# The first phase in an order from a list scheduler, smaller first weight chunks, and the loop's reads in an output bank

## Chip, cores, metric

One core of one Trainium2 chip. The time is device microseconds of one execution; every run in this study was in the fast state, except two of e2's and one of e4b's, which count as slow because they lie over 1.5% above the fastest run of their kernel; ratios leave them out. The profile is one execution, so its span and its waits are one sample; the timed runs are several.

## The reference, cut to what matters

```python
# x: 8 batches x 8 heads x 512 tokens x 64; state: 8 x 8 x 32 x 64
scores  = scale * x @ state.T                    # softmax over the 32 states
xread   = a @ state                              # 512 rows per batch
scores2 = scale * state @ x.T                    # softmax over the 512 tokens
sread   = a2 @ x                                 # 32 rows per batch
tokens  = concat([xread, sread])                 # 8 heads side by side: 512 columns
gate = max(tokens @ w_gate, 0)                   # 512 -> 1536
val  = tokens @ w_val
out  = (gate * val) @ w_out                      # 1536 -> 512
```

The kernel never forms `xread`. For each batch it multiplies the state by the weights (U, 256 rows by 2 x 1536) and multiplies U by the transposed softmax weights (ANS), which saves a product.

## The kernel before

There are five engines in play: TensorE (PE), VectorE (DVE), ScalarE (ACT), GpSimd (POOL) and SyncE (SP, the queue of most DMAs). Each has its own instructions, and the kernel fixes their order. It is written as an explicit order: a list `FIRST` for batches 0, 1 and the preparation of batch 2, then a loop over batches 2 to 7.

A step `("g", b, jf)` is one of the twelve 128-column blocks of gate and value of batch b (four matmuls); `("ge", b, jf)` is its relu on ACT and multiply on DVE. `("u", b, lo, n)` are the U matmuls for n columns, `"ue"` their evictions. `"w"` and `"wo"` load weight chunks, `"xl"` a batch of x, `"st"` states. `"x_bar"` and `"a_bar"` are DMA transposes: of the converted x (xT<-xb), and of the softmax weights (ans<-a_sn). `"sc"`, `"exp"`, `"sum"`, `"mul"` are scores and softmax, `"sr"` the state reads, `"out"` a third of an output tile, `"dummy"` matmuls on a warm-up tile that are meant to keep the clock up.

```python
FIRST = [
    ("st", 1, 2), ("w", 0, 512, ("s", 0)), ("dummy", 7), ("st_cast", 0, 1, "v"), ("st_mm", 0, 1),
    # ... cut
    ("mul", 0, 0, 1, 1, "v"), ("w", 512, 1024, ("v", 0)), ("exp", 0, 1, 0, 1), ("sc", 0, 1, (1,)),
    # ... cut
    ("xl", 3, 0, 8, ("o", 8)), ("u", 0, 1024, 256), ("ge", 1, 7), ("ue", 0, 1024, 256, 0, "a"), ("g", 1, 2),
    # ... cut
    ("u", 1, 1280, 256), ("ge", 1, 9), ("xl", 2, 0, 8, ("v", 512)), ("ue", 0, 1280, 256, 0, "a"), ("sr", 0),
    # ... cut
    ("ue", 2, 512, 512, 3, "v"), ("ue", 2, 512, 512, 1, "v"), ("out", 1), ("conv", 3, 0, 4, "p"), ("u", 2, 1024, 512),
    ("conv", 3, 4, 4, "v"), ("xc", 3, 0, 2, "p"), ("xc", 3, 2, 2, "p"), ("sc", 2, 1), ("sc", 2, 0), ("xl", 4),
    ("x_bar", 3), ("out", 1), ("out", 1), ("exp", 2, 0), ("exp", 2, 1), ("ue", 2, 1024, 512, 1, "a"), ("out", 1),
    ("out", 1), ("sum", 2), ("mul", 2), ("out", 1), ("out", 1), ("a_bar", 2), ("ue", 2, 1024, 512, 0, "a"),
    ("out", 2), ("sr", 2), ("sre", 2), ("ue", 2, 1024, 512, 2, "a"), ("ue", 2, 1024, 512, 3, "a"),
]
# the last entry of a load is its gate: it is issued after that other load has landed.
# ("o", 8): last third of w_out; ("v", 512): w_val columns 512 to 1023.

ps_r = pool("ps_r", 6, PS)      # six rotating PSUM banks
ps_o = pool("ps_o", 2, PS)      # two for output tiles

def sr_mm(b):                   # reads: 32 small matmuls into one rotating bank
    ps = ps_sr[b] = ps_r.tile([128, 130], FP32, name="sr_ps", tag="r")
    # ... cut

# in the loop, batch s + 1 prepared in batch s, at jf == 8:
    sr_mm(s + 1)
    sr_ev(s + 1)
    u_burst(s + 1, 768, 768, "avavav")   # takes all six rotating banks
```

The softmax here doesn't subtract the row's maximum and nothing guards it: scores larger than these inputs give would overflow.

Of the kernel before, what the change touches and what calls it, by code (L numbers as in the profile page):

```python
# [8 lines left out]
FP32 = mybir.dt.float32  # L9
BF16 = mybir.dt.bfloat16  # L10
# [4 lines left out]


FIRST = [
    ("st", 1, 2), ("w", 0, 512, ("s", 0)), ("dummy", 7), ("st_cast", 0, 1, "v"), ("st_mm", 0, 1),
    ("st_ev", 0, 1, "a"), ("dummy", 2), ("conv", 0, 0, 2, "v"), ("conv", 0, 2, 2, "v"), ("xt", 0, 0),
    ("xe", 0, 0, "v"), ("xt", 0, 1), ("dummy", 3), ("conv", 0, 4, 2, "p"), ("conv", 0, 6, 2, "p"), ("sc", 0, 0, (0,)),  # L20
    ("xe", 0, 1, "a"), ("dummy", 1), ("exp", 0, 0, 0, 1), ("dummy", 3), ("sc", 0, 0, (1,)), ("xt", 0, 2),
    ("dummy", 3), ("sum", 0, 0, 0, 1), ("dummy", 3), ("exp", 0, 0, 1, 1), ("xe", 0, 2, "a"), ("xt", 0, 3),
    ("sc", 0, 1, (0,)), ("sum", 0, 0, 1, 1), ("dummy", 7), ("xe", 0, 3, "v"), ("mul", 0, 0, 0, 1, "p"),
    ("mul", 0, 0, 1, 1, "v"), ("w", 512, 1024, ("v", 0)), ("exp", 0, 1, 0, 1), ("sc", 0, 1, (1,)),
    ("sum", 0, 1, 0, 1), ("dummy", 4), ("xl", 1, 0, 4, ("g", 0)), ("exp", 0, 1, 1, 1), ("mul", 0, 1, 0, 1, "v"),
    ("sum", 0, 1, 1, 1), ("dummy", 7), ("conv", 1, 2, 2, "p"), ("mul", 0, 1, 1, 1, "v"), ("st_cast", 1, 2, "v"),
    ("dummy", 6), ("xl", 1, 4, 4), ("at", 0, 0), ("at", 0, 1), ("ae", 0, 0, "a"), ("st_mm", 1, 1), ("u", 0, 0, 256),
    ("ae", 0, 1, "v"), ("dummy", 8), ("st_ev", 1, 1, "v"), ("ue", 0, 0, 256, 1, "v"), ("u", 1, 0, 256),
    ("ue", 0, 0, 256, 0, "a"), ("ue", 1, 0, 256, 0, "a"), ("ue", 1, 0, 256, 1, "v"), ("g", 0, 0),
    ("conv", 1, 0, 2, "v"), ("ge", 0, 0), ("st", 2, 8), ("u", 0, 256, 256), ("conv", 1, 6, 2, "p"),  # L30
    ("conv", 1, 4, 2, "v"), ("ue", 0, 256, 256, 0, "a"), ("xt", 1, 1), ("g", 0, 1), ("w", 1024, 1536), ("xt", 1, 0),
    ("ue", 0, 256, 256, 1, "a"), ("xt", 1, 2), ("xe", 1, 1, "v"), ("ge", 0, 1), ("xe", 1, 0, "a"), ("xt", 1, 3),
    ("g", 0, 2), ("xe", 1, 3, "v"), ("xe", 1, 2, "a"), ("ge", 0, 2), ("sc", 1, 0), ("sc", 1, 1), ("exp", 1, 0),
    ("wo", 0, 4), ("g", 0, 3), ("dummy", 1), ("exp", 1, 1), ("sum", 1, 0), ("dummy", 6), ("mul", 1, 0, 0, 2, "p"),
    ("dummy", 1), ("wo", 4, 8), ("u", 1, 256, 256), ("dummy", 2), ("sum", 1, 1), ("mul", 1, 1, 0, 2, "v"),
    ("dummy", 5), ("ge", 0, 3), ("at", 1, 0), ("dummy", 1), ("at", 1, 1), ("u", 0, 512, 256),
    ("ue", 1, 256, 256, 1, "a"), ("ae", 1, 0, "a"), ("ae", 1, 1, "v"), ("ue", 1, 256, 256, 0, "v"), ("g", 1, 0),
    ("ue", 0, 512, 256, 0, "v"), ("g", 1, 1), ("ge", 1, 0), ("ue", 0, 512, 256, 1, "a"), ("ge", 1, 1), ("wo", 8, 12),
    ("u", 1, 512, 256), ("g", 1, 3), ("g", 0, 4), ("ue", 1, 512, 256, 1, "v"), ("ge", 1, 3), ("ge", 0, 4),
    ("ue", 1, 512, 256, 0, "a"), ("u", 0, 768, 256), ("ue", 0, 768, 256, 1, "v"), ("g", 0, 5),  # L40
    ("ue", 0, 768, 256, 0, "v"), ("u", 1, 768, 256), ("ue", 1, 768, 256, 0, "v"), ("ge", 0, 5), ("g", 1, 5),
    ("ge", 1, 5), ("g", 0, 6), ("ue", 1, 768, 256, 1, "a"), ("ge", 0, 6), ("g", 1, 4), ("g", 1, 7), ("ge", 1, 4),
    ("xl", 3, 0, 8, ("o", 8)), ("u", 0, 1024, 256), ("ge", 1, 7), ("ue", 0, 1024, 256, 0, "a"), ("g", 1, 2),
    ("ge", 1, 2), ("ue", 0, 1024, 256, 1, "a"), ("u", 1, 1024, 256), ("g", 0, 7), ("g", 0, 8),
    ("ue", 1, 1024, 256, 1, "a"), ("xb_alloc", 2), ("ue", 1, 1024, 256, 0, "v"), ("g", 0, 9), ("ge", 0, 7),
    ("ge", 0, 8), ("g", 1, 6), ("g", 1, 9), ("ge", 0, 9), ("st_cast", 2, 8, "v"), ("ge", 1, 6), ("u", 0, 1280, 256),
    ("u", 1, 1280, 256), ("ge", 1, 9), ("xl", 2, 0, 8, ("v", 512)), ("ue", 0, 1280, 256, 0, "a"), ("sr", 0),
    ("g", 1, 8), ("ue", 0, 1280, 256, 1, "a"), ("st_mm", 2, 2), ("ue", 1, 1280, 256, 1, "a"),
    ("ue", 1, 1280, 256, 0, "a"), ("sre", 0), ("sr", 1), ("u_alloc", 2), ("ge", 1, 8), ("st_ev", 2, 2, "a"),
    ("sre", 1), ("g", 0, 11), ("g", 0, 10), ("at_alloc", 3), ("st_mm", 6, 2), ("ge", 0, 11), ("st_mm", 4, 2),  # L50
    ("st_ev", 6, 2, "v"), ("u", 2, 0, 256), ("conv", 2, 4, 4, "p"), ("ge", 0, 10), ("out", 1), ("g", 1, 10),
    ("ge", 1, 10), ("st_ev", 4, 2, "v"), ("g", 1, 11), ("out", 1), ("ge", 1, 11), ("conv", 2, 0, 4, "p"),
    ("xc", 2, 0, 2, "p"), ("xc", 2, 2, 2, "p"), ("at_alloc", 2), ("xb_alloc", 3), ("ue", 2, 0, 256, 0, "a"),
    ("ue", 2, 0, 256, 1, "a"), ("u", 2, 512, 512), ("ue", 2, 512, 512, 0, "a"), ("u", 2, 256, 256),
    ("ue", 2, 256, 256, 1, "a"), ("x_bar", 2), ("ue", 2, 512, 512, 2, "a"), ("out", 1), ("ue", 2, 256, 256, 0, "v"),
    ("ue", 2, 512, 512, 3, "v"), ("ue", 2, 512, 512, 1, "v"), ("out", 1), ("conv", 3, 0, 4, "p"), ("u", 2, 1024, 512),
    ("conv", 3, 4, 4, "v"), ("xc", 3, 0, 2, "p"), ("xc", 3, 2, 2, "p"), ("sc", 2, 1), ("sc", 2, 0), ("xl", 4),
    ("x_bar", 3), ("out", 1), ("out", 1), ("exp", 2, 0), ("exp", 2, 1), ("ue", 2, 1024, 512, 1, "a"), ("out", 1),
    ("out", 1), ("sum", 2), ("mul", 2), ("out", 1), ("out", 1), ("a_bar", 2), ("ue", 2, 1024, 512, 0, "a"),
    ("out", 2), ("sr", 2), ("sre", 2), ("ue", 2, 1024, 512, 2, "a"), ("ue", 2, 1024, 512, 3, "a"),  # L60
]

@with_exitstack
def kernel(
# [9 lines left out]
    nc = tc.nc  # L74
# [38 lines left out]
    tiny = const.tile([128, 1], FP32, name="tiny")  # L113

    xf, xb, xT, e_sn, cs, rc, asn, ANS, U, hsb = ({} for _ in range(10))
    ps_sc, ps_sr, ps_st, ps_x, ps_a, ps_u, ps_g = ({} for _ in range(7))

    def cp(eng, o, i):
        if eng == "a":
# [158 lines left out]


    def sr_mm(b):  # L280
        ps = ps_sr[b] = ps_r.tile([128, 130], FP32, name="sr_ps", tag="r")
        for c in range(NC):
            for s in range(2):
                for j in range(NJ):
                    nc.tensor.matmul(ps[32 * j:32 * j + 32, 65 * s:65 * s + 65], e_sn[b][:, c, s, j],  # L285
                                     xs(b)[:, c, j, 1 + 65 * s:66 + 65 * s],
                                     start=(c == 0 and s == 0), stop=(c == NC - 1), skip_group_check=True)
# [69 lines left out]
                                 ANS[b][:, :, kc], start=(kc == 0), stop=(kc == 1))  # L357
            ps_g[b, jf].append(ps)

    def gv_ev(b, jf):  # L360
        pss = ps_g[b, jf]
        g_sb = gpool.tile([128, 512], BF16, name="g_sb", tag="g_sb")
        nc.scalar.activation(out=g_sb, in_=pss[0], func=AF.Relu)  # L363
        nc.vector.tensor_tensor(out=hsb[b][:, jf], in0=pss[1], in1=g_sb, op=ALU.mult)  # L364

    def gv(b, jf):
        gv_mm(b, jf)
        gv_ev(b, jf)

    def gvs(jf):  # L370
        f0 = jf * 128
# [7 lines left out]
        nc.scalar.activation(out=g_sb[:, 0:nt], in_=ps[:, 0], func=AF.Relu)  # L379
        nc.vector.tensor_tensor(out=hs[0][:, jf], in0=ps[:, 1], in1=g_sb[:, 0:nt], op=ALU.mult)  # L380

    o_ps = [None]

    def out_piece(b, tsub, q):
        if q == 0:
# [3 lines left out]
        src, t0 = (hsb[b], tsub * 128) if b < B else (hs[0], tsub * 128)  # L389
        for jf in range(4 * q, 4 * q + 4):  # L390
            nc.tensor.matmul(o_ps[0], src[:, jf, t0:t0 + 128], wo_sb[:, jf], start=(jf == 0), stop=(jf == NF - 1))  # L391
        if q < 2:
            return
        ps = o_ps[0]
        o_sb = opool.tile([128, d_model], FP32, name="o_sb", tag="o_sb")
        if b < B:
            cp("av"[tsub % 2], o_sb, ps)
# [26 lines left out]
    def outp(n=1):  # L424
        for _ in range(n):
            p = next(pieces, None)
            if p is not None:
                out_piece(*p)


    ctx.enter_context(tc.manual_schedule())
# [17 lines left out]
    for i in range(3):  # L449
# [3 lines left out]
        "dummy": dummies, "w": w_dma, "wo": wo_dma, "st": st_dma,  # L453
        "st_cast": st_cast, "st_mm": st_mm, "st_ev": st_ev, "conv": x_conv, "xc": x_copy, "xt": x_tr, "xe": x_ev,
        "sc": sc_mm, "exp": sc_exp, "sum": nrm_sum, "mul": nrm_mul, "at": a_tr, "ae": a_ev,
        "u": u_mm, "ue": u_ev, "g": gv_mm, "ge": gv_ev, "gv": gv, "sr": sr_mm, "sre": sr_ev, "out": outp,
        "xb_alloc": xb_alloc, "at_alloc": at_alloc, "u_alloc": u_alloc, "x_bar": x_bar, "a_bar": a_bar, "ub": u_burst, "xl": x_dma,
    }
    for name, *args in FIRST:
# [35 lines left out]
    for s in range(2, B):  # L495
        for jf in range(NF):
            gv(s, jf)
            if jf in (3, 9):
                continue
            outp()  # L500
            for k in ((jf - 1, jf) if jf in (4, 10) else (jf,)):
                aux(s + 1, k)
                nxt(s + 2, k)
            if jf in (2, 8):
                if s + 1 < B:
                    if jf == 2:
                        u_alloc(s + 1)
                    else:
                        sr_mm(s + 1)
                        sr_ev(s + 1)  # L510
                    u_burst(s + 1, 768 * (jf // 8), 768, "avavav")
                outp()
    hs.append(xin.tile([128, NF, B * Ns], BF16, name="hs_sb", tag="xf"))
    for jf in range(NF):
# [34 lines left out]
```

## Time and profile before

| | before |
|---|---|
| median time at first | 235.24 us (3 runs, 234.59 to 237.09) |
| span of the profiled run | 234.0 us |
| PE busy | 95% |
| period of the loop, one batch | 23.58 us |
| effective end of the first phase (second loop batch, at 89.12, less one period) | 65.54 us |

The prediction below shows the lines that carry this. In addition, three lines of the timeline of PE give the head of the kernel. The columns are start and length in us, engine, line, operation, out<-in, shapes and count; in brackets is the idle time just before and what ended it.

```profile
13.48 0.30 PE L304 MATMUL u_ps<-wg_sb,stT 64*32 64x256 bf16 x8
...
15.14 1.04 PE L356 MATMUL gv_ps<-ans,U 128*128 128x512 bf16 x4
...
24.25 0.30 PE L304 MATMUL u_ps<-wv_sb,stT 64*32 64x256 bf16 x8 [0.19 <-DMA wv_sb<-in_moe_w_val_dram]
```

The first weights are used at 13.48, the first step runs at 15.14, and at 24.25 the second pair of weight chunks is met. One line of PE's waits belongs to the hole in front of the loop (released by; us in total, times, longest):

```profile
PE gv_ps L356 <- DMA ans<-a_sn: 2.6, 1, 2.6
```

The transposing DMA of batch 2's weights took 3.51 us from 60.18 on, but PE still had an output piece and the state reads to do until 61.1. It stood still for 2.62 us, and the granted clock was 0.50 from 64 to 67 us.

### The profile page before, as it was taken

The numbers are of one execution on the slowest core, as the hardware profiler recorded it, in microseconds if no ns is written. First come the engines' busy times: TensorE is split into PE (matmuls) and PEld (weight loads), VectorE is DVE, ScalarE is ACT, GpSimd is POOL, SyncE is SP. The second block draws the span as 40 slices with busy tenths as digits, with TensorE's granted clock in tenths as the row PEclk, the third lists the DMA queues.
The fourth block names the chain that finished last, engine by engine and source line by source line (L and its number), as shares of the span: only waits on it lengthen the run. The fifth ranks groups of instructions, "written<-read, shape, count | busy, mean of one in ns | idle before, by whom it ended". The sixth has DMA issues, their size and how long they took to land.

```text
span 234.0 us, 4969 instructions
## 1 busy us (share of the span) xinstructions
PE 222.4 (95%) x2000; PEld 111.8 (48%) x2022; DVE 139.2 (59%) x244; ACT 113.4 (48%) x210; POOL 35.0 (15%) x44
## 2 busy tenths in 40 slices
PE   6999999999599999999999999999999999999993
PEld 3856434534244444444444444444444444586553
DVE  5578888574229674867486748675866535442210
ACT  3457678573246354645463647363736353442121
POOL 3356000083600033003300240000000000000000
PEclk9999999999979999999999999999999999999999
DMA  6999995747901674169415761325131111110132
GB/s 190 173 282 195 207 204 160 227 92 224 275 3 45 148 203 105 48 144 202 112 45 125 216 119 48 90 63 125 45 92 50 49 45 45 45 48 31 60 83 99
DMA packets 39463, 27.85 MB, mean 119 GB/s; under 512 B 21136, under 2 KB 35216, under 8 KB 39440
## 3 DMA queue, kind: packets, MB, share of 16 engines
q1 hardware_dynamic: 34688, 22.81, 35.5%
q0 software_dynamic: 4752, 4.72, 12.5%
q8 instruction: 16, 0.26, 0.5%
q14 instruction: 7, 0.06, 0.1%
HBM read 18.35 MB, written 8.91 MB: 116 GB/s over the span
## 4 chain that ended last, share of the span: by engine, by line
PE 77%; DMA 16%; POOL 2%; issue 1%; ACT 1%; DVE 1%; SPq 0%
PE o_ps L391 35%; PE gv_ps L356 30%; DMA wv_sb<-in_moe_w_val_dram 8%; PE gvs_ps L376 4%; PE u_ps L304 4%; DMA xf<-in_x_dram 4%; DMA xT<-xb 2%; DMA ans<-a_sn 1%; PE sc_ps L241 1%; PE o_ps L413 1%; POOL xb L124 1%; DMA st_f<-in_state_dram 1%; ACT g_sb L363 1%; PE sr_ps L285 1%; POOL wg_sb L152 1%
## 5 line engine op out<-in xcount | busy, mean ns | idle before, releaser
L364 DVE TENSOR_TENSOR h_sb<-gv_ps,g_sb 128x512 bf16<-128x512 f32 x96 | 65.5, 689 | 57.5 <-ACT g_sb L363 53.1
L356 PE MATMUL gv_ps<-ans,U 128*128 128x512 bf16 x384 | 95.8, 382 | 2.6 <-DMA ans<-a_sn 2.6
L391 PE MATMUL o_ps<-wo_sb,h_sb 128*128 128x512 bf16 x350 | 91.2, 381 | 2.0 <-issue 1.2
L363 ACT ACTIVATE g_sb<-gv_ps 128x512 bf16<-128x512 f32 x96 | 57.5, 599 | 61.5 <-PE gv_ps L356 60.7
L356 PEld LDWEIGHTS <-U 128*128 128x128 bf16 x384 | 36.1, 98 | 44.3 <-issue 4.4
L391 PEld LDWEIGHTS <-h_sb 128*128 128x128 bf16 x372 | 35.5, 98 | 43.3 <-issue 4.2
L120 ACT CAST U<-u_ps 128x512 bf16<-128x512 f32 x54 | 28.8, 596 | 3.0 <-PE u_ps L304 2.4
L122 DVE CAST U<-u_ps 128x512 bf16<-128x512 f32 x42 | 26.2, 673 | 1.1 <-PE u_ps L304 1.1
L124 POOL CAST xb<-xf 128x1024 bf16<-128x1024 f32 x11 | 11.2, 1040 | 88.5 <-DMA xf<-in_x_dram 88.5
L120 ACT COPY o_sb<-o_ps 128x512 f32<-128x512 f32 (+2 forms) x20 | 10.8, 538 | 20.5 <-PE o_ps L391 18.2
L122 DVE COPY o_sb<-o_ps 128x512 f32<-128x512 f32 (+2 forms) x18 | 11.4, 635 | 12.7 <-ACT o_sb L120 4.5
L252 ACT ACTIVATE e_sn<-sc_ps 128x512 bf16<-128x512 f32 (+1 forms) x18 | 9.7, 549 | 14.6 <-PE sc_ps L241 14.6
L437 PE MATMUL warm_ps<-warm 128*128 128x256 bf16 x70 | 11.7, 316 | 1.2 <-DVE warm L439 1.2
L124 POOL COPY xs<-xb 128x1024 bf16<-128x1024 bf16 x12 | 12.1, 1040 | 1.6 <-DVE xb L122 1.3
L304 PEld LDWEIGHTS <-stT 64*32 64x32 bf16 x576 | 6.7, 90 | 10.0 <-issue 6.9
L304 PE MATMUL u_ps<-wv_sb,stT 64*32 64x256 bf16 (+1 forms) x288 | 11.2, 306 | 0.2 <-DMA wv_sb<-in_moe_w_val_dram 0.2
L258 DVE TENSOR_REDUCE cs<-e_sn 128x32 f32<-128x1024 bf16 (+2 forms) x12 | 10.2, 852 | 1.7 <-ACT e_sn L252 1.7
L380 DVE TENSOR_TENSOR hs_sb<-gvs_ps,g_sb 128x256 bf16<-128x256 f32 x12 | 5.1, 424 | 9.9 <-ACT g_sb L379 9.9
L304 PE MATMUL u_ps<-wg_sb,stT 64*32 64x256 bf16 (+1 forms) x288 | 10.3, 312 | 0.0
L379 ACT ACTIVATE g_sb<-gvs_ps 128x256 bf16<-128x256 f32 x12 | 4.6, 383 | 10.2 <-PE gvs_ps L376 7.8
L264 DVE TENSOR_TENSOR a_sn<-e_sn,rc 128x1024 bf16<-128x1024 bf16 (+2 forms) x10 | 9.4, 944 | 0.1
L437 PEld LDWEIGHTS <-warm 128*128 128x128 bf16 x70 | 7.2, 112 | 3.4 <-DVE warm L439 1.2
(47 smaller groups left out, 102.5 us busy)
## 6 DMA issues: line engine op xcount, KB each, us to landing
out_dram<-o_sb SPq DMA_DIRECT2D x31, 256.0 KB, 2.4
xf<-in_x_dram SPq DMA_DIRECT2D x6, 1024.0 KB, 6.8
wg_sb<-in_moe_w_gate_dram POOLq DMA_DIRECT2D x3, 512.0 KB, 8.0
wv_sb<-in_moe_w_val_dram POOLq DMA_DIRECT2D x3, 512.0 KB, 9.7
wo_sb<-in_moe_w_out_dram POOLq DMA_DIRECT2D x3, 512.0 KB, 13.3
xf<-in_x_dram SPq DMA_DIRECT2D x4, 256.0 KB, 3.5
xf<-in_x_dram SPq DMA_DIRECT2D x2, 512.0 KB, 4.6
out_dram<-o_sb SPq DMA_DIRECT2D x8, 64.0 KB, 1.7
```

Source lines behind the costliest of these rows:

```text
L120: nc.scalar.copy(out=o, in_=i)
L122: nc.vector.tensor_copy(out=o, in_=i)
L124: nc.gpsimd.tensor_copy(out=o, in_=i)
L252: nc.scalar.activation(out=esl(e_sn, b, kc, j2, n).rearrange("p k j n -> p k (j n)"), in_=ps_sc[b, kc].rearrange("p c s j n -> p (c s) j n ...
L258: nc.vector.reduce_sum(out=c, in_=e, axis=AX.X)
L264: en.tensor_tensor(out=a, in0=e, in1=r.to_broadcast(list(e.shape)), op=ALU.mult)
L304: nc.tensor.matmul(ps[32 * j:32 * j + 32, 0:n], stT[r, b, j, 32 * kc:32 * kc + 32], wsb[w][r, j, lo:lo + n], start=(i == 0), stop=True, sk ...
L356: nc.tensor.matmul(ps.rearrange("p (c t) -> p c t", c=NC), U[b][:, kc, w, f0:f0 + 128], ANS[b][:, :, kc], start=(kc == 0), stop=(kc == 1))
L363: nc.scalar.activation(out=g_sb, in_=pss[0], func=AF.Relu)
L364: nc.vector.tensor_tensor(out=hsb[b][:, jf], in0=pss[1], in1=g_sb, op=ALU.mult)
L391: nc.tensor.matmul(o_ps[0], src[:, jf, t0:t0 + 128], wo_sb[:, jf], start=(jf == 0), stop=(jf == NF - 1))
L437: nc.tensor.matmul(wps[:, 0:cols], warm[:, 0:128], warm[:, 0:cols], start=True, stop=True)
```

## The change

Intent: let a model of all engines order the first phase instead of a person, get the first weights sooner by halving the first chunk, and take the loop's state reads out of the banks that U needs. The core of the diff; the list itself is replaced throughout:

```diff
 FIRST = [
-    ("st", 1, 2), ("w", 0, 512, ("s", 0)), ("dummy", 7), ...
+    ("dummy", 9), ("w", 0, 256, ("s", 0)), ("st_cast", 0, 1, "v"), ("st_mm", 0, 1), ("st", 1, 2),
+    ("xl", 1, 0, 2, ("x", 0, 4)), ("xl", 1, 2, 2), ("xl", 1, 4, 2), ("xl", 1, 6, 2), ("dummy", 2),
     ... cut
+    ("st_ev", 1, 1, "a"), ("sc", 0, 1, (1,)), ("dummy", 2), ("w", 256, 512, ("g", 0)), ("exp", 0, 1, 1, 1),
     ... cut
+    ("gr", 0, 6), ("g", 0, 7), ("gm", 0, 6), ("xl", 2, 0, 8, ("v", 1024)), ("gr", 0, 7), ("st", 2, 8), ("g", 1, 3),
     ... cut
+    ("om",), ("sre", 2), ("mul", 2, 0, 0, 2, "p"), ("ue", 2, 1024, 512, 1, "a"), ("conv", 3, 0, 4, "v"), ("g", 1, 7),
+    ("a_bar", 2), ("xc", 3, 0, 2, "v"), ("xc", 3, 2, 2, "p"), ("at_alloc", 3), ("x_bar", 3), ("xl", 4), ("gr", 1, 7),
+    ("g", 1, 6), ("gm", 1, 7), ("gr", 1, 6), ("g", 1, 5), ("gm", 1, 6), ("gr", 1, 5), ("g", 1, 4), ("gm", 1, 5),
     ... cut
 def sr_mm(b):
-    ps = ps_sr[b] = ps_r.tile([128, 130], FP32, name="sr_ps", tag="r")
+    ps = ps_o.tile([128, d_model], FP32, name="sr_ps", tag="o") if b > 2 else \
+        ps_r.tile([128, d_model], FP32, name="sr_ps", tag="r")
+    ps_sr[b] = ps
-def gv_ev(b, jf):      # relu and multiply together
+def gv_relu(b, jf):    # "gr"
+def gv_mult(b, jf):    # "gm"
     ... output pieces ("om") and their evictions ("oe") are split likewise
 # in the loop
     sr_mm(s + 1)
-    sr_ev(s + 1)
-    u_burst(s + 1, 768 * (jf // 8), 768, "avavav")
+    u_mm(s + 1, 768 * (jf // 8), 768)
+    sr_ev(s + 1)
+    # ... then the six evictions
```

The useful work of the first phase is the same: 24 gate/value steps, all of U for batches 0 to 2, 12 output pieces. Dummies fall from 70 to 33.

## The prediction

> **What bounds the kernel now.** I read the page's busy shares first, then the chain of work that ended last in order of time, then the queue waits, then the engine table in stretches, and last the timeline of one period of the loop. The page says TensorE (PE) is the bound: its three big lines make most of the chain, and the clock is at full speed in 39 of 40 slices.
>
> ```profile
> PE 222.4 (95%) x2000; PEld 111.8 (48%) x2022; DVE 139.2 (59%) x244; ACT 113.4 (48%) x210; POOL 35.0 (15%) x44
> PEclk9999999999979999999999999999999999999999
> PE 77%; DMA 16%; POOL 2%; issue 1%; ACT 1%; DVE 1%; SPq 0%
> ```
>
> "PE 95% busy" hides filler: 70 matmuls on a warm-up tile, and modelled ends. The chain is the better guide. Its 16% DMA all lies before 64 us:
>
> ```profile
> 3.79 9.71 DMA wv_sb<-in_moe_w_val_dram
> 14.60 9.60 DMA wv_sb<-in_moe_w_val_dram
> ...
> 37.58 8.94 DMA xf<-in_x_dram
> 46.56 2.03 POOL xb L124 x2
> 48.61 4.55 DMA xT<-xb
> 53.21 0.64 PE sc_ps L241 x16
> 60.18 3.51 DMA ans<-a_sn
> 63.73 1.87 PE gv_ps L356 x4
> 67.50 0.86 PE gv_ps L356 x4
> 72.93 1.73 PE gv_ps L356 x8
> 96.51 1.73 PE gv_ps L356 x8
> 120.09 1.73 PE gv_ps L356 x8
> ```
>
> Three things are to be seen. PE waits for weight chunks up to 24.2 us. Then batch 2 comes late: its x arrives at 46.5, goes through the conversion, the transposing DMA, scores and weights, and PE stands still from 60.18 to 63.73; the first four matmuls afterwards take 1.87 us where four later take 0.86. And from 72.93 on the loop repeats every 23.58 us (96.51 - 72.93 and 120.09 - 96.51). A period's bare matmul time is 48 gate/value and 48 output matmuls at 0.2157 us (0.86 for four), 20.7, plus U 1.8, scores 0.46, state reads 0.36: 23.3. So the loop is at PE's pace already and **only the first phase has time to give**. The third loop batch starts at 89.12 in the chain; one period earlier is 65.54. That is where the first loop batch would have started on an undisturbed PE, and I call it the effective end of the first phase.
>
> The clock explains the 1.87:
>
> ```profile
> 60.00:65.00 5.00, 2.38 (x40) 0.97 (x39) 1.06 (x3) 0.47 (x2) 3.30 (x4) 0.87 0.92 238
> 65.00:70.00 5.00, 4.78 (x33) 2.30 (x33) 1.38 (x2) 1.97 (x5) 0.00 (x0) 0.79 0.01 3
> ```
>
> The third number from the end is the granted clock. Why batch 2 is late stands in the queue's own waits:
>
> ```profile
> SPq L146 <- DMA wo_sb<-in_moe_w_out_dram: 24.4, 1, 24.4
> ```
>
> The loads of x for batches 3 and 2 sit behind a gate on the last output-weight chunk, until 37.03.
>
> **What the Trainium skill says.** (1) "TensorE: Matmul & The Clock Gate", Part 1: some 3.4 us without PE work halves the clock. The trace agrees: 3.5 us of stillness, then 0.50 granted. (2) "DMA: Bandwidth & Descriptors", Queues, rings and completion order: each DMA engine takes turns between its queue rows. So an x load on the SyncE queue takes about half the engines from the weights on the GpSimd queue while both run. The trace before barely tests this. (3) Same page, Specifications: a minimum of 512 B for line rate. A 256-column chunk writes exactly 512 B of bf16 per row, so it should not fall off a cliff; no run here shows it yet.
>
> **The change, part by part.** Both first phases hold the same useful work: 24 gate/value steps of batches 0 and 1, all of U for batches 0 to 2, and 12 output pieces. So I compare when PE reaches the same state, and what it loses afterwards.
>
> *Smaller first chunks.* Before, the 512-column pair lands at 13.5 us and the first U matmul starts at 13.48. Half of it should land near 12. But the first gate/value step also needs batch 0's weights through ScalarE (ACT). The new order puts four U evictions at 0.59, two transposes' copies at 0.59 in ACT's queue ahead of it: 12.4 + 6 x 0.59 = 15.9, against 15.14 before. So the small chunk alone buys nothing for the first step.
>
> *The state "four steps of batch 0 and four U chunks done, waiting for columns 512 and up"* is met by the kernel before at 24.25, when its second pair lands. In the new order the transfers ahead of that pair are the same, less the state of batches 2 to 7 (0.39 MB, some 1.5 us at 250 to 350 GB/s), less the dip near 12.5 us between the gated pairs, plus up to 0.6 us for twice as many small packets (estimate: a 1 KB packet of x took about 45 ns of an engine at 345 GB/s, a 2 KB one of weights 80 ns at 206 GB/s landed). That gives 22 to 22.5 us. **I take 22.3, a gain of 2.**
>
> *From there to the end.* The kernel before used 24.25 to 60.18, 35.9 us, for 20 steps x 0.863 = 17.3, 8 U chunks x 0.34 = 2.7, U of batch 2 2.0, 12 pieces x 0.863 = 10.4, and some 2.2 of state transposes, scores and reads: 34.6, so 1.3 lost. Then came 5.4 us to the effective end at 65.54: the idle wait and the half-speed clock. The new order loads x of batch 2 behind the third weight pair (27.3 us by 22.3 + 5.1 for 1 MB at 206 GB/s), so x is there near 36, its transpose near 41.5, and its scores stand about 45 us in PE's order. After the issue of the last transposing DMA PE still has four steps, four pieces and a U chunk, 7.5 us, against the 3.5 that it takes. **The 5.4 us should vanish.** New losses: the output weights now share the engines with x of batch 2 and the state. Weights alone would end near 35; sharing 1.4 MB moves that to about 39.5, while PE asks for the third part near 39: estimate 0.6 us. ACT's queue at the head, 0.5; ordinary bank waits, 1.3 again plus 0.3. So 22.3 + 34.6 + 2.7 = 59.6, against 65.54: **5.9 us**.
>
> *Reads in an output bank.* In the loop the reads of the next batch take one of the six rotating banks just ahead of the six that U wants, so U waits:
>
> ```profile
> 107.01 0.10 PEld L304 LDWEIGHTS <-stT 64*32 64x32 bf16 x4 [0.27 <-DVE srn L294]
> 106.37 1.04 PE u_ps L304 x32
> 118.34 0.77 PE u_ps L304 x32
> ```
>
> The burst with the reads ahead of it takes 1.04 us, the other 0.77. Five batches x 0.27 = **1.3 us**, on the path since PE is the bound. The output banks: the piece before closes one and its eviction (0.58) is over before the next piece, 1.3 us later, wants it; the reads take the other.
>
> *The split of relu and multiply and of output piece and eviction* costs no instruction. More multiplications on GpSimd (8 against 2, 0.63 us each) are off the path unless its weight issues (0.75 each) hold them up.
>
> Sum: 5.9 + 1.3 = 7.2; 235.2 - 7.2 = **228.0 us**.
>
> **Rivals.** *Output weights or x of batch 2 become the wait.* If turns favour x, the second and third output pieces stand in PE's order with nothing to pass them, and VectorE's order has the conversion of x ahead of multiplies that PE needs. For: DMA busy at full share up to 35 us with the same bytes. Against: one step of slack is there for each. It would cost 2 to 4 us more: 230 to 232. *ACT becomes the bound between 12 and 35 us.* A step costs relu 0.60, multiply 0.69 and one U eviction of 0.6: 1.9 on two engines, 0.95, against PE's 1.03. So tight that a bad split shows. It would leave the state at 24 and some waits: 230 to 231. *Everything but DMA disappears:* fewer stalls than before, 225 to 226. *Cold clock at the head*, since fillers fall from 70 to 33: PE waits near 9.5 to 12 us with little work. A half clock for a few us of steps: 1 us.
>
> **Range and chances.** The 5.4 us is a clear hole that the order fills, and the loop's 1.3 is nearly sure; the 2 us at the head and the contention are my soft terms, plus or minus 3 together. Time 228.0, range 225.0 to 231.5. Two per cent is 230.5; I give 0.80 to faster, 0.17 to the same, 0.03 to slower (a long wait on a late transfer, with a cold clock after it).
>
> **What would show each step.** In the chain: no long wait for the transposing DMA of batch 2 near the loop's start, and the clock at 1.00 there; the first loop step near 58 to 60 us instead of 63.73; the third U pair of columns met near 22; U bursts of 0.77 in both places and a period of 23.3. A PE wait on the output weights between 36 and 41 would show the first rival; ACT busy over 90% from 13 to 30 with PE waiting on its copies the second. I am wrong if the loop's period grows, or if PE's waits before 58 us sum to more than 8 us after the state is met.

## The result, and the profile after

| | before | after |
|---|---|---|
| median, first comparison | 235.42 us (4 runs, 234.59 to 237.09) | 227.28 us (4 runs, 226.2 to 228.69) |
| ratio, 95% interval | | 0.9649 [0.9574, 0.9724] |
| median, on the chip of the experiments | 236.25 us (13 runs, 235.36 to 236.67) | 227.92 us (6 runs, 226.48 to 228.75) |
| ratio, 95% interval | | 0.9641 [0.9614, 0.9667] |
| span of the profiled run | 234.0 us | 224.4 us |

A ratio is the mean time of one kernel's fast runs over the mean of the other's fast runs of the same rounds, so it is not quite the ratio of the medians. The change is faster by 3.5%.

The page of the kernel after (busy shares, clock, and the shares of the chain that ended last):

```profile
PE 214.4 (96%) x1947; PEld 106.1 (47%) x1969; DVE 140.0 (62%) x246; ACT 117.3 (52%) x218; POOL 37.2 (17%) x47
...
PEclk9999999999999999999999999999999999999999
...
PE 88%; DMA 6%; POOL 2%; SPq 1%; issue 1%; DVE 0%; ACT 0%; POOLq 0%
```

DMA's share of the chain fell from 16% to 6%, and no slice shows a lowered clock (its mean is 1.000). "PE 96%" against 95% says almost nothing: the busy share hardly moves when the kernel gets 3.5% shorter. The chain in order of time (start, length, what):

```profile
13.60 9.00 DMA wv_sb<-in_moe_w_val_dram
22.65 0.52 PE u_ps L311 x24
23.17 4.42 PE gv_ps L363 x20
...
45.22 0.57 PE sc_ps L246 x16
...
50.27 3.45 PE gv_ps L363 x16
...
57.84 0.86 PE gv_ps L363 x4
...
63.49 0.77 PE u_ps L311 x32
...
65.23 1.73 PE gv_ps L363 x8
...
75.09 0.77 PE u_ps L311 x32
...
88.54 1.73 PE gv_ps L363 x8
```

From 22.65 to the last output the chain is PE alone. The scores of batch 2 stand at 45.22 instead of 53.21, and the 3.45 us of steps at 50.27 are four steps of batch 1 (`g(1,7)` to `g(1,4)`) that the new order kept back. Most of them lie ahead of the transposing DMA of batch 2's weights, which takes 3.2 us and is issued here (the length is that of the issue):

```profile
52.85 1.26 SPq L280 DMA_TRANSPOSE ans<-a_sn  x1
```

Beside it run the last of the four steps, output pieces and a U chunk: 5.0 us of work up to the first loop step. That step comes at 57.84 instead of 63.73 and takes 0.86 us, at full clock. Both U bursts are 0.77 us. The period is 88.54 - 65.23 = 23.31.

The engine table in stretches, for the two stretches of the hole and of the low clock in the kernel before. The columns are the stretch, its length, busy time of PE, PEld, DVE, ACT and POOL, then granted clock, DMA share and GB/s:

```profile
60.00:65.00 5.00, 4.84 (x59) 2.28 (x58) 2.74 (x4) 3.54 (x8) 1.94 (x2) 1.00 0.76 262
65.00:70.00 5.00, 5.00 (x25) 2.25 (x23) 5.00 (x9) 2.37 (x5) 2.11 (x3) 1.00 0.14 53
```

PE is busy 4.84 of 5 us where it had been 2.38. The head, from the timeline of PE:

```profile
10.10 0.30 PE L311 MATMUL u_ps<-wv_sb,stT 64*32 64x256 bf16 x8 [0.37 <-DMA wv_sb<-in_moe_w_val_dram]
...
14.23 1.03 PE L363 MATMUL gv_ps<-ans,U 128*128 128x512 bf16 x4
...
22.65 0.30 PE L311 MATMUL u_ps<-wv_sb,stT 64*32 64x256 bf16 x8 [1.78 <-DMA wv_sb<-in_moe_w_val_dram]
...
23.10 4.49 PE L363 MATMUL gv_ps<-ans,U 128*128 128x512 bf16 x20
```

With the two traces side by side the gain splits as follows. The effective end of the first phase after is 81.15 - 23.31 = 57.84, from the start of the loop's second batch.

| stretch | before | after | gain |
|---|---|---|---|
| until columns 512 and up are met | 24.25 | 22.65 | 1.6 |
| from there to the effective end of the first phase | 41.3 | 35.2 | 6.1 |
| five periods of the loop | 5 x 23.58 | 5 x 23.31 | 1.3 |
| sum | | | 9.0 |

The end of the last matmul moved by the same 9.0 (230.20 to 221.21); the other 0.6 of the 9.6 between the spans lies in the last output's transfer. The timed medians differ by 8.1 and 8.3 only: the profiled run of the kernel after is its fastest, 226.2 us, while that of the kernel before, 235.82 us, is near its median. The experiments show what its other runs meet.

### The profile page after: what moved, and what is told of

Read it like the earlier page. It is cut to its first block, busy times and chain, and to the rows that moved or that the text cites. A ratio compares the mean times of both kernels' runs of the same rounds, so it can differ in the third digit from the quotient of the medians.

```text
span 224.4 us, 4881 instructions
## 1 busy us (share of the span) xinstructions
PE 214.4 (96%) x1947; PEld 106.1 (47%) x1969; DVE 140.0 (62%) x246; ACT 117.3 (52%) x218; POOL 37.2 (17%) x47
## 4 chain that ended last, share of the span: by engine, by line
PE 88%; DMA 6%; POOL 2%; SPq 1%; issue 1%; DVE 0%; ACT 0%; POOLq 0%
PE o_ps L400 38%; PE gv_ps L363 36%; PE u_ps L311 5%; PE gvs_ps L385 5%; DMA wv_sb<-in_moe_w_val_dram 4%; DMA st_f<-in_state_dram 2%; PE sc_ps L246 1%; PE o_ps L425 1%; PE sr_ps L292 1%; SPq L151 1%; POOL wg_sb L157 1%; PE stT_ps L184 1%; POOL xs L129 1%; POOL a_sn L269 1%; POOL wv_sb L157 0%
## 5 line engine op out<-in xcount | busy, mean ns | idle before, releaser
L363 PE MATMUL gv_ps<-ans,U 128*128 128x512 bf16 x384 | 94.3, 379 | 0.1
L127 DVE CAST U<-u_ps 128x512 bf16<-128x512 f32 x41 | 25.7, 673 | 3.7 <-PE u_ps L311 3.5
L129 POOL CAST xb<-xf 128x1024 bf16<-128x1024 f32 x10 | 10.2, 1043 | 83.8 <-PE gv_ps L363 38.2
L311 PE MATMUL u_ps<-wv_sb,stT 64*32 64x256 bf16 (+1 forms) x280 | 9.6, 309 | 2.2 <-DMA wv_sb<-in_moe_w_val_dram 2.2
L263 DVE TENSOR_REDUCE cs<-e_sn 128x8 f32<-128x256 bf16 (+2 forms) x15 | 10.6, 708 | 0.5 <-ACT e_sn L257 0.3
L129 POOL COPY xs<-xb 128x1024 bf16<-128x1024 bf16 x10 | 10.4, 1065 | 1.0 <-DVE xb L127 0.7
L311 PEld LDWEIGHTS <-stT 64*32 64x32 bf16 x560 | 5.9, 90 | 9.8 <-issue 8.0
L454 PE MATMUL warm_ps<-warm 128*128 128x256 bf16 x33 | 6.7, 321 | 1.2 <-DVE warm L456 1.2
L246 PEld LDWEIGHTS <-xT 128*128 128x128 bf16 x128 | 5.8, 98 | 4.2 <-ACT xT L125 0.7
L246 PE MATMUL sc_ps<-stT,xT 128*128 128x64 bf16 x128 | 6.9, 193 | 0.4
```

The lines of the kernel that those rows point to most:

```text
L127: nc.vector.tensor_copy(out=o, in_=i)
L129: nc.gpsimd.tensor_copy(out=o, in_=i)
L246: nc.tensor.matmul(ps_sc[b, kc][:, c, :, j2], xT[b][:, c, j], stT[:, b, j].rearrange("p (s n) -> p s n", s=2), start=True, stop=True)
L263: nc.vector.reduce_sum(out=c, in_=e, axis=AX.X)
L311: nc.tensor.matmul(ps[32 * j:32 * j + 32, 0:n], stT[r, b, j, 32 * kc:32 * kc + 32], wsb[w][r, j, lo:lo + n], start=(i == 0), stop=True, sk ...
L363: nc.tensor.matmul(ps.rearrange("p (c t) -> p c t", c=NC), U[b][:, kc, w, f0:f0 + 128], ANS[b][:, :, kc], start=(kc == 0), stop=(kc == 1))
```

## The experiments

Twelve kernels ran on one chip and share its runs of the kernel before. Differences "in us" below are differences of ratios times 236.2 us.

| run | median us | ratio to before, 95% |
|---|---|---|
| after_again | 227.92 | 0.9641 [0.9614, 0.9667] |
| e1_reads_back | 228.38 | 0.9679 [0.9654, 0.9704] |
| e2_before_reads | 235.53 | 0.9934 [0.9893, 0.9976] |
| e3_x_early | 234.29 | 0.9928 [0.9896, 0.9961] |
| e4_x_early_order | 236.15 | 1.0004 [0.9965, 1.0042] |
| e4b_order_only | 237.32 | 1.0027 [0.9992, 1.0063] |
| e9_both_early | 233.12 | 0.9869 [0.9845, 0.9893] |
| e5_whole_chunk | 230.19 | 0.9751 [0.9729, 0.9772] |
| e11_before_small | 240.99 | 1.0204 [1.0184, 1.0223] |
| e6_state_early | 227.48 | 0.9644 [0.9620, 0.9668] |
| e7_fill | 227.45 | 0.9630 [0.9611, 0.9648] |
| e8_fill_sooner | 227.42 | 0.9622 [0.9602, 0.9642] |

Medians are over all runs of a kernel. Of e2's six runs two are slow, of e4b's six one.

### The reads: e1 takes them back, e2 moves them alone

e1 is the kernel after with its reads in a rotating bank for every batch:

```diff
-    ps = ps_o.tile([128, d_model], ...) if b > 2 else ps_r.tile([128, d_model], ...)
-    ps_sr[b] = ps
+    ps = ps_sr[b] = ps_r.tile([128, d_model], FP32, name="sr_ps", tag="r")
```

> The kernel after with one part undone: the state reads of batches 3 to 7 take one of the six rotating banks again. Theory (the U burst waits for the reads' eviction whenever they stand ahead of it in the same ring): the loop's period goes from 23.31 back to 23.58 us, the burst behind the reads from 0.77 to 1.04, five times, so 1.3 us slower than the kernel after (about 0.97 of the kernel before). Rival (in the new order, with reads evicted behind the U matmuls in the program, the bank matters little): within 0.3 us of the kernel after, period 23.3. A third possibility: the eviction of the reads now stands behind U matmuls in program order, so the wait could also be longer than 0.27.

e2 is the kernel before with the changed `sr_mm` and the loop's U matmuls ahead of `sr_ev`, nothing else:

```diff
     sr_mm(s + 1)
-    sr_ev(s + 1)
-    u_burst(s + 1, 768 * (jf // 8), 768, "avavav")
+    u_mm(s + 1, 768 * (jf // 8), 768)
+    sr_ev(s + 1)                       # at jf == 8
+    # ... then the six evictions
```

> The kernel before with only the loop's part of the change: the reads of batches 3 to 7 in an output bank and their eviction put behind the U matmuls in the program; the first phase as it was. Theory: period 23.31, 5 x 0.27 = 1.3 us faster than the kernel before (ratio 0.994); the hole at 60 us stays. Rival: the first phase's order and the loop's part work only together (the ring of banks is shared), then 0 to 0.5 us.

The chain of e1 has one burst behind the reads and one without them:

```profile
75.71 1.04 PE u_ps L309 x32
...
87.68 0.77 PE u_ps L309 x32
```

And e2's chain has, behind the reads:

```profile
82.69 0.77 PE u_ps L306 x32
```

e1's period is 23.57 us and e2's 23.31. In time e1 gives 0.9 us back (0.9679 - 0.9641) and e2 wins 1.6; the traces' 5 x 0.27 = 1.3 lies between the two. The times alone would not show it: e1's interval overlaps with that of the kernel after, and with the two runs of e2 that count as slow, whose clocks are no lower than the others', its gain would be about 0.9 us. The bursts and periods show it, in either first phase, and e1 changes nothing but the bank. In e2 the hole in front of the loop stays (PE waits 2.6 us for the transposed weights of batch 2).

### The hole: e3, e4b, e4, e9

The kernel before loads x of batch 3 ahead of that of batch 2, both behind the last output weights. e3 only turns them round, and gates batch 2 on the third pair of weight chunks, as the kernel after does:

```diff
-    ("xl", 3, 0, 8, ("o", 8)), ("u", 0, 1024, 256), ...
+    ("xl", 2, 0, 8, ("v", 1024)), ("u", 0, 1024, 256), ...
-    ("u", 1, 1280, 256), ("ge", 1, 9), ("xl", 2, 0, 8, ("v", 512)), ...
+    ("u", 1, 1280, 256), ("ge", 1, 9), ("xl", 3, 0, 8, ("o", 8)), ...
```

> The kernel before with the x of batch 2 issued ahead of that of batch 3 and gated on the third weight pair instead of waiting behind the last output weights; orders of all engines else as they were. If the late x alone makes the hole at 60.18 to 63.73 us: x of batch 2 lands near 38 instead of 46.5 and the hole and the cold clock go, 4 to 5.4 us faster. If the order makes it (scores stand behind a U chunk, and sum, multiply and the transposing DMA behind output copies): the scores' wait of 0.47 us goes, the hole stays near 3.5, at most 1 us faster. I expect the second.

e4b leaves the loads and only moves batch 2's softmax and transpose ahead of the work of batch 3 and the output pieces; e4 does both:

```diff
-    ("conv", 3, 0, 4, "p"), ("u", 2, 1024, 512), ("conv", 3, 4, 4, "v"), ..., ("sc", 2, 1), ("sc", 2, 0), ("xl", 4),
-    ("x_bar", 3), ("out", 1), ("out", 1), ("exp", 2, 0), ("exp", 2, 1), ..., ("out", 1),
-    ("out", 1), ("sum", 2), ("mul", 2), ("out", 1), ("out", 1), ("a_bar", 2), ...
+    ("sc", 2, 1), ("sc", 2, 0), ("exp", 2, 0), ("exp", 2, 1),
+    ("conv", 3, 0, 4, "p"), ("u", 2, 1024, 512), ("sum", 2), ("mul", 2), ("a_bar", 2),
+    ("conv", 3, 4, 4, "v"), ("xc", 3, 0, 2, "p"), ("xc", 3, 2, 2, "p"), ("xl", 4),
+    ("x_bar", 3), ("out", 1), ("out", 1), ..., then the other output pieces
```

> The kernel before with x as late as it was, but with scores, exponentials, sum, multiply and transposing DMA of batch 2 moved ahead of the last U chunk, the conversion of batch 3 and the last output pieces in every engine's order. Late x sets the scores at 53.2 us as before; the chain behind them gets shorter by the waits on output copies: the DMA is issued near 57.5 instead of 60.2, PE waits 1 to 1.5 us for it instead of 3.5 and the clock stays: 2 to 4 us faster. If late x is all that counts: PE only waits earlier, at the scores, and nothing is gained (within 1 us).

> Both of the previous edits together on the kernel before: x of batch 2 early, and its chain ahead in the order. If the 5.4 us of the hole are what the change's first phase gained and both are needed: 4 to 5.4 us faster than the kernel before, the first loop step near 59 us, clock 1.00. If the kernel after gained by something else: under 3 us.

e9 loads both x early (batch 3 without a gate, behind batch 2) and puts the conversion and transpose of batch 3's x first, then batch 2's softmax and transpose, then the output pieces:

```diff
-    ("xl", 3, 0, 8, ("o", 8)), ... ("xl", 2, 0, 8, ("v", 512)), ...
+    ("xl", 2, 0, 8, ("v", 1024)), ... ("xl", 3, 0, 8), ...
+    ("conv", 3, 0, 4, "p"), ("conv", 3, 4, 4, "v"), ("xc", 3, 0, 2, "p"), ("xc", 3, 2, 2, "p"), ("x_bar", 3), ("xl", 4),
+    ("sc", 2, 1), ("sc", 2, 0), ("exp", 2, 0), ("exp", 2, 1), ("u", 2, 1024, 512), ("sum", 2), ("mul", 2), ("a_bar", 2),
+    then all output pieces
```

> The kernel before with x of batch 2 gated on the third weight pair, x of batch 3 right behind it, batch 3's conversion and transposing DMA ahead of batch 2's chain, and that chain ahead of the last U chunk and output pieces. The two order experiments before only moved the hole: batch 3's transposed x came late instead of batch 2's weights. If the hole is these two chains and nothing else: no PE wait over 1 us from 25 us on, clock 1.00, 4 to 5 us faster than the kernel before. If something else holds PE there: under 2 us.

e3 wins 1.7 us [0.9 to 2.5 from the interval], but its profiled run, at 236.0 us one of its slower ones, still has the hole (PE waits 2.8 us). From its chain:

```profile
60.32 3.50 DMA ans<-a_sn
```

That is where it stood in the kernel before (60.18). The x is there earlier, but the scores of batch 2 still stand behind the same work in PE's order (53.25, against 53.21). e3's six runs split: three at clock 1.0 took 233.7 to 234.0 us, three at 0.993 took 234.6 to 236.2. So e3 shows a gain and not cleanly where it comes from.

e4b and e4 win nothing. Their PE waits name the reason (engine, line, releaser: us in total, times, longest); e4b, then e4:

```profile
PE sc_ps L242 <- DMA xT<-xb: 3.3, 1, 3.3
```

```profile
PE sc_ps L242 <- DMA xT<-xb: 3.1, 1, 3.1
```

The wait on batch 2's weights is gone, and one of the same size on the transposed **x of batch 3** has taken its place. That x is needed right behind the loop's first step and output piece, and its transpose, issued behind batch 2's, took 7.27 us in e4's chain. There are two transposing chains in front of the loop; hurrying one alone puts the other on the path.

e9 hurries both and wins 3.1 us. What is left of the hole, in its PE waits and in its table of stretches:

```profile
PE gv_ps L356 <- DMA ans<-a_sn: 1.3, 1, 1.3
```

```profile
60.00:65.00 5.00, 3.65 (x56) 1.96 (x56) 1.75 (x4) 1.65 (x3) 4.05 (x4) 1.00 0.86 221
```

The clock is at 1.00 there, and the anchor in the loop that is 72.93 before comes at 69.28, 3.65 us sooner. It still has 1.3 us of idle time: the transpose of batch 2's weights was issued at 56.63 and took 5.06 us, and PE had work for 3.75 us of it. In the kernel after the transpose took 3.2 us and PE had 5.0 us of work. So e9's wait may be due to missing work or to the slower transpose; no run separates the two.

### The first chunk: e5 takes it back, e11 makes it alone

e5 is the kernel after with the whole first chunk:

```diff
-    ("dummy", 9), ("w", 0, 256, ("s", 0)), ...
+    ("dummy", 9), ("w", 0, 512, ("s", 0)), ...
-    ("dummy", 2), ("w", 256, 512, ("g", 0)), ("exp", 0, 1, 1, 1), ...
+    ("dummy", 2), ("exp", 0, 1, 1, 1), ...
```

> The kernel after with the first weight columns as one 512-column pair instead of two 256-column pairs, everything else as it is. Theory (the second step waits for the pair of columns 512 to 1023, at 22.65 us, whatever came first): the first U matmul is later by some 2 us (10.1 to 12 or more), the first steps too, but PE has 1.78 us of waiting at 20.9 to absorb it; the third wait moves by less than 1 us; total within 1 us of the kernel after, either way. Rival (the small first chunk is where the first phase's gain comes from): 2 us slower or more.

e11 is the kernel before with the split chunk:

```diff
-    ("st", 1, 2), ("w", 0, 512, ("s", 0)), ...
+    ("st", 1, 2), ("w", 0, 256, ("s", 0)), ...
-    ("w", 512, 1024, ("v", 0)), ...
+    ("w", 256, 512, ("g", 0)), ("w", 512, 1024, ("v", 0)), ...
```

> The kernel before with only the small first chunks: 256 columns, then 256, then as before; its orders unchanged. In the order of the kernel before, PE does batch 0's attention ahead of its first U chunk and needs columns 512 and up from 24.2 us, so the small chunk should give less than 1 us (or cost up to 0.6 us, more packets). If small chunks are worth the 2.5 us that the kernel after lost without them whatever the order: 2 us faster or more.

e5 is 2.6 us slower than the kernel after (0.9751 - 0.9641). Its timeline of PE:

```profile
14.87 0.41 PE L311 MATMUL u_ps<-wv_sb,stT 64*32 64x256 bf16 x8 [3.78 <-DMA wv_sb<-in_moe_w_val_dram]
...
19.50 1.03 PE L363 MATMUL gv_ps<-ans,U 128*128 128x512 bf16 x4
```

The value weights are met at 14.87, where the kernel before had the whole pair by 13.5, though they were issued at the same 3.79 us; here x of batch 1 is issued beside them from 6.48 us on, there at 10.92. That this is the reason was not tested by a run of its own. PE stands still for 3.78 us, the granted clock is 0.50 from 15 to 18 us, and the first step runs at 19.50 instead of 14.23. Of these 5.3 us some 3.2 are left at the loop: its first step is at 61.03 against 57.84.

e11 is 4.8 us *slower* than the kernel before (its interval starts at 1.0184, so at a threshold of 2% the verdict is unclear). In its order PE wants the second U chunk soon after the first, and now its columns arrive later: a wait of 2.82 us and then half a clock. The first loop step is at 68.25 instead of 63.73. Its timeline and its table of stretches:

```profile
19.08 0.41 PE L304 MATMUL u_ps<-wv_sb,stT 64*32 64x256 bf16 x8 [2.82 <-DMA wv_sb<-in_moe_w_val_dram]
```

```profile
20.00:23.00 3.00, 3.00 (x18) 1.89 (x16) 1.12 (x2) 1.99 (x5) 0.00 (x0) 0.50 1.24 207
```

So the same edit is worth +2.6 in one order and -4.8 in the other. It belongs to the order and can't be judged, or carried over, alone.

### The bytes moved behind the weights: e6

The prediction gave 1.5 us of the head to loading the states of batches 2 to 7 later. e6 loads them early again in the kernel after:

```diff
-    ("xl", 1, 6, 2), ("dummy", 2), ...
+    ("xl", 1, 6, 2), ("st", 2, 8), ("dummy", 2), ...
-    ("gr", 0, 7), ("st", 2, 8), ("g", 1, 3), ...
+    ("gr", 0, 7), ("g", 1, 3), ...
```

> The kernel after with the state of batches 2 to 7 (0.39 MB) loaded right behind the x of batch 1, as the kernel before did, instead of behind the x of batch 2. Theory (the head gained because these bytes no longer stand before the weights of columns 512 to 1023): these columns are met some 1.5 us later, at 24.2 instead of 22.65, and the kernel is 1 to 1.5 us slower than the kernel after, since PE has no slack from there to the loop. Rival (the wait there is hidden later, since the x of batch 2 gains what the weights lose): within 0.4 us.

In its profile columns 512 and up are met at 23.56 instead of 22.65, and the first loop step is at 58.80 instead of 57.84, so the bytes may delay the weights. The time does not show it: 0.9644 against 0.9641. The kernel after's own profile of another run meets them at 23.25 (next part), so a single profile is no evidence for 0.9 us at this place. The 1.5 us are not confirmed. Leaving out the runs with a lowered clock of 0.990 to 0.992 changes nothing: 227.2 to 227.6 us in e6, 226.5 to 227.8 in after_again.

### The wait that is left at 21 us: after_again, e7, e8

> The kernel after, unchanged, timed on the same chip and in the same rounds as the next three, and as a second look at its head: its runs so far lie between 226.2 and 228.7, and its profile was taken from the fastest. Expected ratio to the kernel before 0.963 to 0.968; the wait for columns 512 to 1023 ends between 22.6 and 23.8 us.

after_again is the kernel after unchanged. Its profiled run is its slowest, 228.75 us, and shows what the fast one of the first comparison had been spared:

```profile
23.25 0.30 PE L311 MATMUL u_ps<-wv_sb,stT 64*32 64x256 bf16 x8 [1.94 <-DMA wv_sb<-in_moe_w_val_dram]
...
23.78 6.06 PE L363 MATMUL gv_ps<-ans,U 128*128 128x512 bf16 x20
```

```profile
25.00:26.00 1.00, 1.00 (x4) 0.42 (x3) 0.23 (x1) 0.45 (x1) 0.00 (x0) 0.50 1.22 200
```

A wait of 1.94 us instead of 1.78, and behind it the clock at 0.50: five steps take 6.06 us instead of 4.49, so some 1.6 us are lost, and the first loop step is at 60.09 instead of 57.84. Three of its six runs have a mean clock of 0.992, like this one, and took 228.08 to 228.75; the three at 0.997 to 0.999 took 226.48 to 227.76.

e7 puts steps of batch 1 whose columns are there already into that wait; e8 puts more of them there, and issues batch 2's transpose of weights sooner:

```diff
 # e7
-    ("sr", 1), ("ae", 1, 0, "a"), ("u", 0, 512, 256), ("sre", 1), ("u", 0, 768, 256),
+    ("sr", 1), ("ae", 1, 0, "a"), ("g", 1, 1), ("g", 1, 3), ("gr", 1, 1), ("u", 0, 512, 256), ("sre", 1), ("gm", 1, 1),
+    ("gr", 1, 3), ("u", 0, 768, 256), ("gm", 1, 3),
     # ... and g(1,2), g(1,0) ahead of ("u", 0, 1280, 256)
 # e8, on top of e7
     # g(1,0) ahead of ("u", 0, 768, 256), g(0,0) in place of four dummies,
     # mul and a_bar of batch 2 ahead of the conversion of batch 3
```

> The kernel after with steps of batch 1 that need only columns 0 to 511 (four of them) moved ahead of the two U chunks that wait for weights: two ahead of the wait for columns 512 to 1023 (1.78 us of PE idle), two ahead of columns 1024 and up. If PE's work is the only bound behind that wait: 1.2 to 1.7 us faster than the kernel after. If batch 2's chain (its x transposed lands at 45.1, its weights at 56.3, PE is there at 45.15 and 57.7) is the next bound with 0.1 to 1.3 us of slack: 0 to 0.7 us faster, with new waits for the transposed x and for the transposed weights near the loop's start. I expect the second.

> A try at a version that beats both: the kernel after with the filled waits of the previous fill (now three steps of batch 1 around the wait for columns 512 to 1023, one ahead of columns 1024 and up), step 0 of batch 0 put into a slot where PE ran four filler matmuls and idled near 15.5 us, and the multiplies of batch 2 ahead of the conversion of batch 3 on GpSimd so that the next chain does not become the bound. If PE work is all that counts behind 17 us: first loop step 1 to 1.5 us earlier than in the kernel after, ratio near 0.958. If evictions (ACT and VectorE in order) take over: no gain, with PE waits on U copies or on the copies of batch 1's weights.

Both do what they are for: no run of either has a clock at or below 0.996, e7's profile has no PE wait on weights at all, and the runs lie close together (226.86 to 227.66, and 226.52 to 227.54, against 226.48 to 228.75). But the ratios, 0.9630 and 0.9622, overlap with 0.9641. Part of the gain comes back as new waits, in e8's list of PE waits:

```profile
PE gv_ps L364 <- ACT ans L126: 0.6, 1, 0.6
PE gv_ps L364 <- ACT U L126: 0.6, 1, 0.6
...
PE sc_ps L247 <- DMA xT<-xb: 0.6, 1, 0.6
```

With PE's gap closed, ACT's copies come due too late. e8 has the lowest median, 227.42. It and e7 were the steadier in these few runs; that either is faster than the change as given is not shown.

## Why the prediction was right

The time of 228.0 was met: 227.28 at first, 227.92 in the runs beside the experiments. The terms behind it did not all hold.

**The hole, 5.4 us: right in what happened, too simple in its cause.** There is no wait on batch 2's weights, the clock is 1.00, and the first loop step is at 57.84, just ahead of the predicted 58 to 60; the scores stand at 45.22 (predicted 45). But the prediction put the hole down to the late x of batch 2. Early x alone is worth 1.7 us, hurrying batch 2's softmax alone nothing. What it lacked is that batch 3's transposed x must come early too (e4b and e4 against e9). It also counted on 7.5 us of PE work behind the issue of the last transposing DMA, against 3.5 that it takes. The trace has 5.0 us from the issue at 52.85, since PE had done three of the four steps by then, and the transpose took 3.2. That this work was needed is argued from e9's 1.3 us and not shown.

**The head, 2.0 us: about the size, partly the wrong reasons.** The state in question was met at 22.65 and 23.25 in two runs, against 24.25: 1.6 and 1.0. The sentence that failed is "the small chunk alone buys nothing for the first step". The prediction expected the first step at 15.9; it came at 14.23, and e5 puts the chunk at 2.6 us in the new order. What it missed: the first pair is in use at 10.10, not at "near 12"; and it compared with the old arrival at 13.5, while in the new order the whole chunk would have arrived at 14.87, with x of batch 1 beside it. The other reason, 1.5 us for the states' bytes, found no support in time (e6).

**New losses, 2.7 us: too high for the good run, and of another kind in the rest.** The stretch from the state to the effective end took 35.2 us, only 0.6 above the 34.6 of bare work. PE did not wait on the output weights at all, where 0.6 had been set. Instead a half clock behind the wait at 21 us cost some 1.6 us in after_again's profile, and four of the ten runs of the kernel after, three of them in after_again, have the lower mean clock of 0.992 that goes with it. The prediction named a cold clock, but near 9.5 to 12 us; there it stayed at 1.00.

**The loop, 1.3 us: right**, by mechanism and size: bursts of 0.77 in both places and a period of 23.31 (predicted 23.3), 0.9 and 1.6 us in e1 and e2.

**The rivals.** Output weights or x of batch 2 as the wait: not seen in the kernel after. ACT as the bound: not seen there either, but near, since ACT's copies are what PE waits for as soon as e8 fills the gap. "Everything but DMA disappears", 225 to 226: the best run, 226.2, is close to it.

**Slips in its working.** It took the 3.51 us of the transposing DMA for PE's stillness. PE worked on until 61.1 and waited 2.62, so of the 6.7 us that it counts as 1.3 before the hole and 5.4 in it, some 2.3 lie before and 4.4 in it; the sum stays. The batch at 89.12 is the loop's second, not its third. The bare period of 23.3 us has U at 1.8, which holds the 0.27 of the bank's wait; two bursts of 0.77 make it 23.1, so the loop was less near to PE's pace than it seemed. And 22.3 + 5.1 is 27.4.

So the errors partly cancelled, and that the middle fell on 228 is partly luck. The losses were set too high by 2 us for the profiled run. The six runs without the lower clock took 226.2 to 227.8 us and the four with it 228.1 to 228.8.

**What stays open.** What the half clock in the hole of the kernel before costs: of its 13 runs three had a mean clock of 1.0 and, at 235.83 to 236.18, were no faster. Where e3's 1.7 us lie. Why e6's later loop start costs nothing in time. And e9 plus e2, 3.1 and 1.6 us, which were not run together, make 4.7 of the 8.5 that the whole change is worth (1 - 0.9641); the remaining 3.8 were not taken apart into head, kept-back steps and chunk.

## What to carry to other kernels

When PE stands still in front of a loop, list all the chains that must arrive there, not only the one that came last: hurrying one by itself moved the wait to its neighbour at no gain. Independent matmuls kept back for the time in which those transfers run should help (argued here, not tested). The size of a first transfer and the order behind it are one decision: the same split gained 2.6 us in one order and lost 4.8 in the other. And take more than one profile before a term below 2 us is believed, for a run-dependent half clock behind a short wait is of that size.

## What the Trainium skill lacked or had wrong

- "TensorE: Matmul & The Clock Gate", Part 1, gives a cold clock after an idle window of about 3.4 us and says the window runs freely. What it lacks is how little idleness inside a window is enough. Here a wait of 1.94 us, with PE busy 1.31 us of the 3 us from 20 to 23, was followed by a granted clock of 0.50; the same kernel with a wait of 1.78 us and 1.22 us busy in the same stretch kept 1.00. The kernel before lost its clock after 2.62 us. So a kernel should not leave waits of 2 us on the assumption that only 3.4 us count.
- "DMA: Bandwidth & Descriptors", DMA Transpose (X-bar), has no durations for transposes inside SBUF beside other traffic (elsewhere the page has only a bandwidth). Here the 512 KB transpose of x took 4.55 us in the kernel before and 7.27 in e4, and the 256 KB one of the weights 3.51 in the kernel before and 5.06 in e9.
- "DMA: Bandwidth & Descriptors", Queues, rings and completion order, has the turns between queue rows, and e5 fits it; it lacks a worked case of what they cost. Here the 512-column pair was met at 14.87 us with x of batch 1 issued beside it from 6.48 on, against 13.48 in the kernel before, which held that x until 10.92.
